# Cluster attention, then token mixing: every transfer on one queue, in order of time

## The chip, the cores and the metric

The kernel runs on one core of a Trainium2 chip. A core has a matrix engine (TensorE, PE in the profile), a vector engine (VectorE, DVE), a scalar engine (ScalarE, ACT), a general engine (GpSimd, POOL) and a sequencer for transfers (SyncE, SP). SP and ACT both issue DMA transfers in this program. The metric is the device time of one execution in microseconds (us), the median of several runs.

## The reference

```python
mask   = q_assign[:, :, :, None] == k_assign[:, :, None, :]   # nearest of 16 centroids
scores = where(mask, (q @ k.T) / sqrt(D), -1e9)               # B=4, H=8, S=768, D=64
x      = softmax(scores) @ v                                  # regrouped to (4, 768, 512)

theta  = x @ w_theta
zr, zi = x * cos(theta), x * sin(theta)
y      = w_tok_r @ zr + w_tok_i @ zi                          # over the 768 tokens
u      = x + y
out    = u + maximum(u @ w_ch, 0)
```

## The kernel before, in words

The kernel first computes attention, in 16 pairs of heads, and writes x, transposed, to DRAM (`xT_d[b]`). Then it does the token mixing batch by batch. A batch has 6 tiles of 128 tokens; tile number n = 6 b + t runs from 0 to 23. Every float32 matrix is split into a high and a low part, and a product is made of three matmuls.

For each tile there is a *theta*: `theta_parts` splits a column block `xs` of x into `xh` (ACT) and `xl`; `theta_angle` multiplies it by w_theta on TensorE (tile `tp`); `theta_turn` reduces the angle on VectorE (`kk`, `rab`), takes an Abs on ACT, transposes a block `xb` of x into `xn`, and starts the load of the next `xb` (`load_blocks`, four transfers of many short pieces); then come two sines on ACT and two products with `xn` on VectorE. `load_columns` loads the next `xs`.

Batches 0 and 1 are *plain* (`PLAIN = 2`): `mix` multiplies a tile of z by the tiles of the token weights, and `channel_plain` does the channel mix. While they run, `make_forms` loads the kept weights (`w_d`) into two buffers `ws`, makes for each of the 6 weight tiles seven sums of halves, splits each into a high and a low part in two other `ws` buffers, and writes them to DRAM (`w_f`, called wf).

Batches 2 and 3 use these sums: `mix_forms` makes seven products for a tile (m in the order 4, 3, 1, 5, 2, 6, 7), once for the first 256 columns of z (tiles 0 to 5) and once for the second (tiles 5 to 0). The seven sums of a weight tile have to lie in SBUF for it. Tiles 1 to 3 get places of the plain weights (`wr`, `wi`). Tile 0 gets the four `ws` buffers (m = 4, 3, 1, 5) and three plain places; tile 5 gets the same seven places after tile 0, tile 4 the four buffers `u` of the channel mix. So tiles 0, 4 and 5 are loaded again in every batch. `split_z` prepares z for it: VectorE makes three sums (`zt`) and a difference, ACT casts both parts to their high halves, POOL subtracts for the low halves (`zf`). The second half of z goes by DRAM: `keep_turned` writes it (`zd`), `load_z` reads it back (`zb`).

What sets the order: in the attention and in batches 2 and 3 the instructions of each engine stand in the order in which the code issues them (`in_order`). In the plain batches a scheduler orders them by its own estimate of time, and transfers of batch 2 can be moved in among those of the plain batches if their data allow it. An engine takes its instructions strictly in order, so a transfer that has to wait holds all behind it on its issuing engine, computing ones too if that is ACT. The transfers of SP and ACT share eight completion counters in turn: an issue also waits until the last transfer on its counter has landed.

Of the kernel before, what the change touches and what calls it, by code (L numbers as in the profile page):

```python
# [31 lines left out]
AHEAD = 2  # L32
# [9 lines left out]
def kernel(  # L42
# [19 lines left out]
    nc = tc.nc  # L62
    B, H, D, S = qT.shape
    P = 128
    NP = H // 2
    NT = S // P
    C = cent.shape[0] // H
    DM = w_theta.shape[0]
# [6 lines left out]
    xT_d = [dram.tile([P, NP, S], F32, name=f"xT_d{b}") for b in range(B)]  # L75
# [104 lines left out]
    w_d = {(t, x): dram.tile([P, S], F32, name=f"wd{t}{x}") for t in range(NT) for x in "ri"}  # L180
# [11 lines left out]
    for x in range(3):  # L192
        x = (NPAIR + x) % 3
# [67 lines left out]
    def f(ap):  # L261
        return ap.bitcast(F32)
# [60 lines left out]
    def turn_one_hot(pi, n):  # L323
        ot = bank(f"ot{pi}{n}").bitcast(BF16)[:, 0:S]
        for t in range(NT):
            nc.tensor.transpose(
                out=ot[:, t * P:(t + 1) * P], in_=ohp[:, n, t].rearrange("p j c -> p (j c)"), identity=identb)
        return ot
# [267 lines left out]
    def run(gen):  # L596
        for _ in gen:
            pass
# [29 lines left out]
    def behind(x):  # L628
        return tc.issue_after(x.ins) if x is not None else nullcontext()
# [8 lines left out]
    def load_blocks(n):  # L638
        if n == B * NT:
            return  # L640
        b, t = divmod(n, NT)
        xb = blocks[n] = ma[0].tile([P, DM], F32, tag="xb", name=f"xb{n}")


        for a in range(P // 32):
            src = xT_d[b][:, :, t * P + 32 * a:t * P + 32 * a + 32]
            (nc.sync if n < 2 else nc.scalar).dma_start(  # L647
                out=xb[32 * a:32 * a + 32].rearrange("c (n m r) -> c n m r", n=NP, m=P // 32),
                in_=src.rearrange("(m c) n r -> c n m r", c=32))

# [144 lines left out]
    while u <= NUT or todo:  # L795
# [8 lines left out]
        if 0 <= u < NUT:  # L804
            both(score_products, u, exps)
            if u == 0:
# [4 lines left out]
                for n, x in ((1, "mk"), (0, "mq")):  # L811
                    nc.scalar.activation(
                        out=st[1][x], in_=turn_one_hot(1, n), func=AF.Identity,
# [45 lines left out]
    spares = [spare_pool.tile([P, S], F32R, name=f"ws{x}") for x in range(3)]  # L859
# [19 lines left out]
    def load_x(b):  # L879
        xT = xts[b] = mx.tile([P, NP, S], F32, tag="xT", name=f"xT{b}")  # L880
        if b == 0:

            for p in range(NP):
                nc.sync.dma_start(out=xT[:, p], in_=xT_d[b][:, p])
        else:
            nc.sync.dma_start(out=xT, in_=xT_d[b])
# [31 lines left out]
    columns = {}  # L918

    def load_columns(n):  # L920

        b, t = divmod(n, NT)
        if 0 < b < B:
            columns[n] = mxs.tile([P, NCT, P], F32, tag="xs", name=f"xs{n}")
            with tc.issue_after(last_load[0].ins):
                nc.scalar.dma_start(out=columns[n], in_=xT_d[b][:, :, t * P:(t + 1) * P])

    PLAIN = 2
    turning = {}
# [31 lines left out]
    z_d = {}  # L961
# [13 lines left out]
    def keep_turned(b, t, rab):  # L975
        zs[b, t] = rab
        z_d[b, t] = dram.tile([P, 2, DM // 2], F32, tag=f"z{t}", name=f"zd{b}_{t}", bufs=2)
        nc.scalar.dma_start(out=z_d[b, t], in_=rab[:, :, DM // 2:DM])

    def rotate(b, t, rab, xn):  # L980
        if b < PLAIN:
# [20 lines left out]
    last_mix = [None]  # L1002
# [37 lines left out]
    HD = DM // 2  # L1040
# [7 lines left out]
    def make_forms():  # L1048

        for t in range(NT):  # L1050
            for x, k in enumerate("ri"):
                nc.sync.dma_start(out=f(spares[x]), in_=w_d[t, k])
            part = [f(spares[x])[:, c:c + HS] for x in range(2) for c in (0, HS)]
            yield
            for x, m in enumerate(ORDER):
                to = spares[2 + (7 * t + x) % 2]
                hi, lo = to[:, 0:HS], to[:, HS:S]
                p, op, q = W_SUM[m]
                src = part[p]
                if op is not None:  # L1060
                    src = mzb.tile([P, 2, HD], F32, tag="zb", name=f"sum{t}_{m}").rearrange("p x n -> p (x n)")[:, 0:HS]
                    nc.vector.tensor_tensor(out=src, in0=part[p], in1=part[q], op=op)
                nc.scalar.copy(out=hi, in_=src)  # L1063
                nc.gpsimd.tensor_tensor(out=lo, in0=src, in1=f(hi), op=ALU.subtract)  # L1064
                nc.sync.dma_start(out=w_f[t][:, m - 1], in_=f(to))
                yield

    def load_forms(t, ms=ORDER):
        for m in ms:
            nc.sync.dma_start(out=f(forms[t][m]), in_=w_f[t][:, m - 1])  # L1070
# [3 lines left out]
    def load_z(b, t):  # L1074

        if t >= 0:
            second[t] = mzb.tile([P, 2, HD], F32, tag="zb", name=f"zb{b}_{t}")
            nc.sync.dma_start(out=second[t], in_=z_d.pop((b, t)))

    def split_z(b, t, h):  # L1080

        src = zs.pop((b, t)) if h == 0 else second.pop(t)
        n = src.shape[2] // P
        z = mz.tile([P, 2, 2 * DM], F32R, tag="z", name=f"zf{b}_{t}_{h}")
        hi, lo = z[:, 0], z[:, 1]
        c, s = src[:, 0], src[:, 1]
        sums = mzt.tile([P, 3 * P], F32, tag="zt", name=f"zt{b}_{t}_{h}")
        nc.vector.tensor_tensor(out=sums[:, 0:HD], in0=c[:, 0:HD], in1=s[:, 0:HD], op=ALU.add)  # L1088
        nc.vector.tensor_tensor(out=sums[:, HD:3 * P], in0=c[:, 0:P], in1=s[:, P:HD], op=ALU.add)
        parts = src.rearrange("p x (m n) -> p (x m) n", n=P)  # L1090
        nc.vector.tensor_tensor(
            out=parts[:, 1:n + 1:n - 1], in0=src[:, :, P:HD], in1=src[:, :, 0:P], op=ALU.subtract)
        for cols, of in ((slice(0, 3 * P), sums), (slice(3 * P, 7 * P), src[:, :, 0:HD])):
            h_, l_ = (x[:, cols] for x in (hi, lo))
            if len(of.shape) == 3:
                h_, l_ = (x.rearrange("p (x n) -> p x n", x=2) for x in (h_, l_))
            nc.scalar.copy(out=h_, in_=of)  # L1097
            nc.gpsimd.tensor_tensor(out=l_, in0=of, in1=f(h_), op=ALU.subtract)  # L1098
        return hi, lo
# [101 lines left out]
    late_weights, new_forms = late(), make_forms()  # L1201
    for n in range(PLAIN * NT):
        b, t = divmod(n, NT)
        theta(*divmod(n + AHEAD, NT))
        if b == 0:
            weights_after[0] = splits[n + 1]
            next(late_weights, None)
        mix(b, t)
        if 0 < n < PLAIN * NT - 1 and t < NT - 1:
            for _ in range(5 if b == 0 else 6):  # L1210
                next(new_forms, None)
        if n == PLAIN * NT - 2:
            run(new_forms)
            load_forms(0)
            load_forms(1)
        if t == NT - 1:
            if b == PLAIN - 1:
                load_forms(2)
                load_forms(3)
            channel_plain(b)  # L1220
            load_x(b + 1)
    us = [u_tile(f"u{x}") for x in range(4)]
# [15 lines left out]
    def turn(n):  # L1238
        if n < last:
            theta_turn(n)  # L1240
            sines(turning[n][4])
# [7 lines left out]
    for b in range(PLAIN, B):  # L1249
        for t in range(NT - 1):  # L1250
            n = b * NT + t
            done(n + 1)
            angle(n + 2)
            before(n + 3)
            now, z = z, split_z(b, t + 1, 0)
            mix_forms([(t, now)], t == 0, False)
            if t < 4:
                load_forms(*((4, ORDER[:4]), (4, ORDER[4:]), (5, ORDER[:4]), (5, ORDER[4:]))[t])
            if t == 2 and b > PLAIN:
                load_x(b)  # L1260
            turn(n + 2)
            if t == NT - 2:
                load_z(b, 5)
        n = b * NT + NT - 1
        load_z(b, 4)
        done(n + 1)
        now, z = z, split_z(b, 5, 1)
        load_z(b, 3)
        mix_forms([(5, now)], False, True)
        angle(n + 2)  # L1270
        add_products(b, 0, 0)
        now, z = z, split_z(b, 4, 1)
        load_z(b, 2)
        add_products(b, 0, 1)
        before(n + 3)
        for t in (5, 4, 3, 2, 1, 0):
            mix_forms([(t, now)], t == 5, t == 0)
            if t == 5:
                load_forms(0, ORDER[:4])
            if t == 4:  # L1280
                load_forms(0, ORDER[4:])
            if t > 1:
                now, z = z, split_z(b, t - 2, 1)
                load_z(b, t - 4)
            else:
                now = z
            if t == 5:
                turn(n + 2)
            if t == 4:
                done(n + 2)  # L1290
                split_u_part(b, 0, us, nc.vector)
        for k in range(2):
            add_products(b, 1, k)
        split_u_part(b, 1, us, nc.vector)
        if b + 1 < B:
            z = split_z(b + 1, 0, 0)
        channel(b, us)
# [53 lines left out]
```

## Time and profile before

| | us |
|---|---|
| median of 3 runs (lowest, highest) | 856.79 (854.31, 858.82) |
| the profiled execution: its own time | 860.01 |
| its span, first to last instruction | 858.2 |
| mean granted TensorE clock | 0.958 |
| attention, up to its last row sums on TensorE | 0 to 451.4 |
| plain batches, from the first product of `mix` | 453.4 to 646 |
| batch 2 (theta 14 to the end of its channel mix) | 646 to 760.5 |
| batch 3 | 760.5 to 858.2 |

A line of the timeline gives start, duration, engine, line of the code, operation, output tile and input tiles, sizes and count. In square brackets stands how long the engine sat idle before, and what ended that. ACTq and SPq are the issuing of transfers by ACT and SP. PEclk, or "granted clock", is the share of its full clock that TensorE got. The lines that matter are shown in the prediction.

### The profile page before, as it was taken

The numbers are of one execution on the slowest core, as the hardware profiler recorded it, in microseconds if no ns is written. First come the engines' busy times: TensorE is split into PE (matmuls) and PEld (weight loads), VectorE is DVE, ScalarE is ACT, GpSimd is POOL, SyncE is SP. The second block draws the span as 40 slices with busy tenths as digits, with TensorE's granted clock in tenths as the row PEclk, the third lists the DMA queues.
The fourth block names the chain that finished last, engine by engine and source line by source line (L and its number), as shares of the span: only waits on it lengthen the run. The fifth ranks groups of instructions, "written<-read, shape, count | busy, mean of one in ns | idle before, by whom it ended". The sixth has DMA issues, their size and how long they took to land. (4 is left out here: it accounts for less than half of the span.)

```text
span 858.2 us, 14512 instructions
## 1 busy us (share of the span) xinstructions
PE 785.1 (91%) x5316; PEld 578.1 (67%) x5316; DVE 635.1 (74%) x797; ACT 415.0 (48%) x835; POOL 564.2 (66%) x345
## 2 busy tenths in 40 slices
PE   9999999999999999997999895999983969995798
PEld 6656666656656666664657784888872858994698
DVE  7688999999999999995858997474654357634654
ACT  3566667667667666663554445333522233213320
POOL 3677898899999998995664946835662244223350
PEclk9999999999999999998999998899986898897999
DMA  3113433334544334424537747489969646167242
GB/s 131 53 52 97 129 110 104 104 117 153 159 134 128 102 115 158 149 89 173 156 81 216 221 118 220 156 296 303 323 230 365 239 104 194 41 249 229 69 171 74
DMA packets 115235, 135.38 MB, mean 158 GB/s; under 512 B 62226, under 2 KB 81308, under 8 KB 114780
## 3 DMA queue, kind: packets, MB, share of 16 engines
q1 hardware_dynamic: 55932, 120.82, 41.6%
q10 hardware_dynamic: 59232, 13.64, 7.5%
q8 instruction: 42, 0.69, 0.3%
q14 instruction: 29, 0.24, 0.1%
HBM read 96.99 MB, written 37.33 MB: 157 GB/s over the span
## 5 line engine op out<-in xcount | busy, mean ns | idle before, releaser
L485 ACT ACTIVATE at<-sc 128x384 f32<-128x384 f32 x384 | 173.8, 493 | 100.4 <-PE m L409 53.2
L431 DVE TENSOR_REDUCE nm<-m 128x1 f32<-128x768 f32 x192 | 180.4, 947 | 29.9 <-PE m L409 23.9
L496 POOL TENSOR_TENSOR acc<-at,at 128x768 f32<-128x768 f32 x64 | 126.5, 1976 | 40.4 <-ACT at L485 40.4
L409 PE MATMUL m<-hk,hq 64*128 64x384 f32 x384 | 147.8, 385 | 0.2 <-DVE nm L431 0.2
L557 PE MATMUL av<-at,vt 128*64 128x384 f32 x768 | 146.7, 501 | 0.2 <-ACT xt L572 0.2
L496 POOL TENSOR_TENSOR acc<-acc,at 128x768 f32<-128x768 f32 x64 | 131.8, 2059 | 13.4 <-ACT at L485 11.4
L409 PE MATMUL m<-mk,mq 64*128 64x384 f32 x384 | 128.6, 335 | 0.1
L409 PE MATMUL sc<-hq,hk 64*128 64x384 f32 x384 | 117.4, 392 | 7.3 <-ACT at L485 7.1
L409 PEld LDWEIGHTS sc<-hq,hk 64*128 64x128 f32 x384 | 55.4, 184 | 69.7 <-ACT at L485 25.0
L409 PE MATMUL sc<-mq,mk 64*128 64x384 f32 x384 | 97.3, 336 | 0.0
L409 PE MATMUL sc<-hq,lk 64*128 64x384 f32 x384 | 97.3, 335 | 0.0
L409 PE MATMUL sc<-lq,hk 64*128 64x384 f32 x384 | 97.0, 335 | 0.0
L557 PEld LDWEIGHTS av<-at,vt 128*64 128x64 f32 x768 | 46.8, 136 | 59.6 <-issue 54.5
L1098 POOL TENSOR_TENSOR zf<-zt,zf 128x384 fp32r<-128x384 f32 x24 | 26.2, 1091 | 70.2 <-ACT zf L1097 65.1
L409 PEld LDWEIGHTS m<-hk,hq 64*128 64x128 f32 x384 | 70.8, 184 | 2.0 <-DVE nm L431 1.4
L409 PEld LDWEIGHTS m<-mk,mq 64*128 64x128 f32 x384 | 71.4, 186 | 0.8 <-DVE mk L374 0.4
L500 DVE TENSOR_TENSOR acc<-acc,acc 128x768 f32<-128x768 f32 x30 | 63.5, 2118 | 0.0
L1064 POOL TENSOR_TENSOR ws<-sum,ws 128x384 fp32r<-128x384 f32 x30 | 33.9, 1135 | 39.7 <-ACT ws L1063 39.6
L1025 PE MATMUL y<-wr_hi,z 128*128 128x512 f32 (+1 forms) x192 | 51.5, 340 | 4.6 <-ACT z L991 3.7
L409 PEld LDWEIGHTS sc<-mq,mk 64*128 64x128 f32 x384 | 54.6, 185 | 0.0
L409 PEld LDWEIGHTS sc<-lq,hk 64*128 64x128 f32 x384 | 54.5, 186 | 0.0
L409 PEld LDWEIGHTS sc<-hq,lk 64*128 64x128 f32 x384 | 54.4, 185 | 0.0
(222 smaller groups left out, 1779.1 us busy)
## 6 DMA issues: line engine op xcount, KB each, us to landing
wf<-ws SPq DMA_DIRECT2D x42, 384.0 KB
ws<-wf SPq DMA_DIRECT2D x20, 384.0 KB
vt<-in_v_dram SPq DMA_DIRECT2D x16, 384.0 KB
rb<-sd SPq DMA_DIRECT2D x32, 192.0 KB
xT_d<-xt SPq DMA_DIRECT2D x16, 384.0 KB
out_dram<-ot SPq DMA_DIRECT2D x32, 192.0 KB
rawq<-in_qT_dram SPq DMA_DIRECT2D x15, 384.0 KB
rawk<-in_kT_dram SPq DMA_DIRECT2D x15, 384.0 KB
```

The lines of the kernel that those rows point to most:

```text
L409: nc.tensor.matmul(out, lhsT=stat[r, cols], rhs=mov[r, over], start=start, stop=stop)
L431: nc.vector.tensor_reduce(out=s["nm", a][:, j, i // 2:i // 2 + 1], in_=s["m", j][:, :, 0:HS], op=ALU.max, axis=AX.XY, negate=True)
L485: last_exp[0] = nc.scalar.activation(out=s["at", a, i][:, j], in_=s["sc", j], func=AF.Exp, scale=SCALE)
L496: last_acc[0] = nc.gpsimd.tensor_tensor(out=s["acc", a, x], in0=prev, in1=at, op=ALU.add)
L500: nc.vector.tensor_tensor(out=s["acc", a, 0], in0=s["acc", a, 0], in1=s["acc", a, 1], op=ALU.add)
L557: nc.tensor.matmul(s["av"][64 * j:64 * j + 64], lhsT=s["vt"][:, i, j, :], rhs=s["at", a, i][:, j], start=(i == 0), stop=(i == NT - 1))
L1025: last_mix[0] = nc.tensor.matmul(y_at(d, c0, c1), lhsT=zz[:, d * P:(d + 1) * P], rhs=ww[:, c0:c1], start=first and lead, stop=last, skip_g ...
L1064: nc.gpsimd.tensor_tensor(out=lo, in0=src, in1=f(hi), op=ALU.subtract)
L1098: nc.gpsimd.tensor_tensor(out=l_, in0=of, in1=f(h_), op=ALU.subtract)
```

## The change

All transfers of the mixing are issued by SP: the blocks `xb`, the columns `xs` and the second half of z (`zd`) were issued by ACT before. The loads of the weights' sums are written tile by tile from the fourth tile of batch 1 on (tile 1, then 0 and 2, then 3), with the column loads ahead of them, and not all at its end. The loads of kept weights into the `ws` buffers are placed behind the last matmul issued by `mix` so far. In batches 2 and 3 the next theta's turn is written behind the load of z, and `split_z` handles the four parts of which the first products are made ahead of the three sums.

```diff
@@ load_blocks
-            (nc.sync if n < 2 else nc.scalar).dma_start(
+            nc.sync.dma_start(
@@ load_columns
-        if 0 < b < B:
+        if 0 < b < B and n not in columns:
...
-                nc.scalar.dma_start(out=columns[n], in_=xT_d[b][:, :, t * P:(t + 1) * P])
+                nc.sync.dma_start(out=columns[n], in_=xT_d[b][:, :, t * P:(t + 1) * P])
@@ keep_turned
-        nc.scalar.dma_start(out=z_d[b, t], in_=rab[:, :, DM // 2:DM])
+        nc.sync.dma_start(out=z_d[b, t], in_=rab[:, :, DM // 2:DM])
@@ make_forms
-                nc.sync.dma_start(out=f(spares[x]), in_=w_d[t, k])
+                with behind(last_mix[0]):
+                    nc.sync.dma_start(out=f(spares[x]), in_=w_d[t, k])
@@ split_z
-        for cols, of in ((slice(0, 3 * P), sums), (slice(3 * P, 7 * P), src[:, :, 0:HD])):
+        for cols, of in ((slice(3 * P, 7 * P), src[:, :, 0:HD]), (slice(0, 3 * P), sums)):
@@ the loop over the plain tiles
-        if n == PLAIN * NT - 2:
-            run(new_forms)
-            load_forms(0)
-            load_forms(1)
+        if b == PLAIN - 1:
+            if t == NT - 2:
+                run(new_forms)
+            if t > 2:
+                load_columns(n + AHEAD + 2)
+            if t == NT - 2:
+                load_forms(0)
+            if t > 2:
+                load_forms(t - 2)
         if t == NT - 1:
-            if b == PLAIN - 1:
-                load_forms(2)
-                load_forms(3)
             channel_plain(b)
@@ the loop over batches 2 and 3
-            turn(n + 2)
             if t == NT - 2:
                 load_z(b, 5)
+            turn(n + 2)
```

Three places show what this does to the order. The first is ACT in batch 2, from the Abs of theta 15 to the casts of z for tile 3 of the products. Before:

```order
L670 ACTIVATE rab_3_7870<-rab_3_7870 128x512
L647 DMA xb_7987<-xT_d_62 32x16x32 x4
L965 ACTIVATE rab_3_7870<-rab_3_7870 128x512
L965 ACTIVATE rab_3_7870<-rab_3_7870,halfpi 128x512
L978 DMA zd_3_7996<-rab_3_7870 256x1x256
L926 DMA xs_8011<-xT_d_63 128x4x128
L936 CAST xh_5_8014<-xs_7940 128x512
L1097 CAST zf_3_0_8020<-zt_3_0_8021 128x384
L1097 CAST zf_3_0_8020<-rab_3_7870 128x512
```

Now (the numbers of lines are one higher behind the changed place):

```order
L670 ACTIVATE rab_3_7870<-rab_3_7870 128x512
L965 ACTIVATE rab_3_7870<-rab_3_7870 128x512
L965 ACTIVATE rab_3_7870<-rab_3_7870,halfpi 128x512
L936 CAST xh_5_8014<-xs_7940 128x512
L1098 CAST zf_3_0_8020<-rab_3_7870 128x512
L1098 CAST zf_3_0_8020<-zt_3_0_8021 128x384
```

The six issues are gone from ACT, and the cast of the 512 columns stands ahead of the cast of the sums.

The second place is SP where batch 1 ends and batch 2 begins. wf_6124 to wf_6129 are the sums of weight tiles 0 to 5; ws_6084, 6085, 6086 and 6121 are the four buffers, for m = 4, 3, 1 and 5 of tile 0. Before:

```order
L1065 DMA wf_6129<-ws_6086 128x768
L1065 DMA wf_6129<-ws_6121 128x768
L1173 DMA out_dram<-ot_1_0_7782 128x384
L1070 DMA ws_6084<-wf_6129 128x768
L1173 DMA out_dram<-ot_1_1_7797 128x384
L1070 DMA ws_6085<-wf_6129 128x768
L1070 DMA ws_6086<-wf_6124 128x768
L1070 DMA ws_6121<-wf_6124 128x768
```

Now:

```order
L1066 DMA wf_6129<-ws_6121 128x768
L1174 DMA out_dram<-ot_1_0_7784 128x384
L1071 DMA ws_6086<-wf_6124 128x768
L1174 DMA out_dram<-ot_1_1_7799 128x384
L647 DMA xb_7916<-xT_d_62 32x16x32
L978 DMA zd_2_7925<-rab_2_7839 256x1x256
L926 DMA xs_7940<-xT_d_62 128x4x128
L1071 DMA ws_6121<-wf_6124 128x768
```

The two loads of tile 5 that stood ahead of tile 0's third and fourth load are further back, and zd and xs of theta 14 and 17 stand ahead of the fourth.

The third place is SP at the begin of batch 3. Before:

```order
L1173 DMA out_dram<-ot_1_3_8619 128x384
L1070 DMA u_7832<-wf_6128 128x768 x2
L1070 DMA u_7833<-wf_6128 128x768 x2
L1070 DMA u_7834<-wf_6128 128x768 x2
L1070 DMA u_7835<-wf_6128 128x768
L1070 DMA ws_6084<-wf_6129 128x768
L1070 DMA ws_6085<-wf_6129 128x768
```

Now:

```order
L1174 DMA out_dram<-ot_1_3_8619 128x384
L926 DMA xs_8635<-xT_d_63 128x4x128
L1071 DMA u_7834<-wf_6128 128x768 x2
L1071 DMA u_7835<-wf_6128 128x768 x2
L647 DMA xb_8683<-xT_d_63 32x16x32 x4
L978 DMA zd_2_8692<-rab_2_8280 256x1x256
L926 DMA xs_8707<-xT_d_63 128x4x128
L1071 DMA u_7836<-wf_6128 128x768 x2
L1071 DMA u_7837<-wf_6128 128x768
L647 DMA xb_8754<-xT_d_63 32x16x32 x4
L978 DMA zd_3_8763<-rab_3_8637 256x1x256
L1071 DMA ws_6084<-wf_6129 128x768
```

The loads of tiles 4 and 5 went out in one run before; now the small transfers of each theta stand between them, and zd holds what is behind it until VectorE has made its products.

## The prediction

> **What bounds the kernel now.** The page comes first: TensorE is busy 91% of the span, and nearly all that it lacks is in the last third. The windows, one for each stage of the last two batches, show where:
>
> ```profile
> PE 785.1 (91%) x5316; PEld 578.1 (67%) x5316; DVE 635.1 (74%) x797; ACT 415.0 (48%) x835; POOL 564.2 (66%) x345
> 646.00:671.00 25.00, 10.46 (x35) 8.66 (x34) 8.59 (x15) 3.64 (x7) 4.28 (x4) 0.60 1.04 373
> 671.00:713.00 42.00, 33.81 (x155) 29.88 (x155) 23.52 (x38) 14.24 (x25) 15.36 (x13) 0.91 0.46 127
> 713.00:760.50 47.50, 44.49 (x235) 43.34 (x234) 28.60 (x51) 12.15 (x21) 17.56 (x15) 0.93 0.42 128
> 760.50:796.40 35.90, 25.26 (x120) 22.50 (x120) 14.25 (x26) 9.09 (x17) 9.72 (x8) 0.86 0.76 251
> 796.40:858.20 61.80, 52.09 (x279) 49.03 (x277) 34.98 (x62) 13.79 (x24) 17.98 (x16) 0.97 0.30 106
> ```
>
> The columns are length, busy time of PE, PEld, DVE, ACT, POOL, granted clock, DMA share, GB/s. No engine is full in these stages, so waits set the time. Next the timeline of TensorE: the first five rows give the price of undisturbed work, the others are the stalls and edges (the last row is the end of the chain of waits).
>
> ```profile
> 736.59 0.68 PE L1113 MATMUL four<-wi_lo,zf 128*128 128x384 f32 x3
> 740.23 0.68 PE L1113 MATMUL four<-ws,zf 128*128 128x384 f32 x3
> 743.87 0.51 PE L1164 MATMUL four<-u,wch_hi 128*128 128x384 f32 x2
> 760.51 1.08 PE L659 MATMUL tp<-wth_hi,xh 128*128 128x512 f32 x4
> 763.27 0.69 PE L1113 MATMUL four<-ws,zf 128*128 128x384 f32 x3
> ...
> 655.46 1.33 PE L1113 MATMUL four<-ws,zf 128*128 128x384 f32 x3 [6.50 <-DMA ws<-wf]
> 665.71 2.67 PE L1113 MATMUL y<-ws,zf 128*128 128x384 f32 x6 [7.96 <-DMA ws<-wf]
> 668.18 1.17 PE L1113 MATMUL y<-wr_hi,zf 128*128 128x384 f32 x3
> 671.06 1.35 PE L659 MATMUL tp<-wth_hi,xh 128*128 128x512 f32 x4
> 684.36 1.17 PE L659 MATMUL tp<-wth_hi,xh 128*128 128x512 f32 x4
> 693.61 1.16 PE L659 MATMUL tp<-wth_hi,xh 128*128 128x512 f32 x4 [2.19 <-DVE rab L667]
> 728.52 0.62 PE L1113 MATMUL four<-wi_hi,zf 128*128 128x384 f32 x2 [1.73 <-ACT zf L1097]
> 784.17 2.08 PE L659 MATMUL tp<-wth_hi,xh 128*128 128x512 f32 x4 [10.64 <-ACT xh L936]
> 795.04 0.69 PE L1113 MATMUL four<-wr_lo,zf 128*128 128x384 f32 x3
> ...
> 534.00 1.01 PE L1164 MATMUL cp<-uh,wch_hi 128*128 128x384 f32 x2 [7.41 <-ACT uh L1156]
> ...
> 854.33 0.56 DVE ot L1171
> ```
>
> One tile's seven products cost 740.23 - 736.59 = 3.64 us, one theta (tp) 763.27 - 760.51 = 2.76, one channel mix 760.51 - 743.87 = 16.64. Against these, stage by stage:
> - 646.0 to 671.0: 25.0 us for a theta and one tile (6.4): 18.6 lost, to loads of the sums of weights (ws<-wf).
> - to 713.0: 42.0 for four thetas and five tiles (29.2): 12.8 lost.
> - to 760.5: 47.5 for a theta, six tiles, a channel mix (41.2): 6.3 lost.
> - to 795.04: 34.5 for four thetas and three tiles (22.0): 12.5 lost.
> - to TensorE's end, at 854.3: 59.3 for nine tiles and a channel mix (49.4): 9.9 lost. The output behind it ends at 858.2.
>
> That is 60 us. Now ScalarE in the second and fourth of these stages:
>
> ```profile
> 685.78 0.64 ACT L670 ACTIVATE rab<-rab 128x512 f32<-128x512 f32 x1 [1.08 <-DVE rab L668]
> 686.34 2.66 ACTq L647 DMA_DIRECT2D xb<-xT_d  x4
> 689.05 0.63 ACT L965 ACTIVATE rab<-rab 128x512 f32<-128x512 f32 x1 [2.62 <-DMA xb<-xT_d]
> ...
> 774.43 0.63 ACT L965 ACTIVATE rab<-rab 128x512 f32<-128x512 f32 x1 [8.02 <-DMA ws<-wf]
> 782.81 0.59 ACTq L926 DMA_DIRECT2D xs<-xT_d  x1
> 783.50 0.62 ACT L936 CAST xh<-xs 128x512 fp32r<-128x512 f32 x1 [7.83 <-DMA zd<-rab]
> ```
>
> ScalarE itself issues the transfers xb, zd and xs. The four xb stand between the Abs and the sines and take 2.66 us. Before 774 an issue also has to wait for a load of weights to land, so the sines start 8.02 late, and the next xh, behind zd and xs, another 7.83: the 10.64 us of TensorE at 784.
>
> **The change part by part.** *Issues moved from ACT to SP (xb, xs, zd).* Six DMA issues a tile leave ScalarE.
>
> Second stage: from theta to theta 693.61 - 684.36 = 9.25 us. Work alone would be 2.76 + 3.64 = 6.40; the loop of waits (VectorE's reduction, Abs, xb issue, sines, VectorE's products) is what takes 9.25. Less 2.66 it is 6.6, barely over TensorE. The issue of xs (0.59) and that of zd lie beside VectorE's work and are worth nothing by themselves. Four periods with some disturbance bring 42.0 to 33: -9, between 0 (the loop finds another wait) and -12.8 (TensorE full).
>
> Third stage: the one theta inside it loses its xb issue too, behind which the cast zf stood that TensorE waits for at 728.52. That stall is the stage's only long one, so -4 of 6.3; ends +2 (the zt buffer, below) and -6.3.
>
> Fourth stage: ScalarE no longer waits there for foreign transfers. The 10.64 and the slow matmuls behind (2.08 instead of 1.08) go: 34.5 to 23, -11.5, ends -5 (half of the wait remains as late xs) and -12.5.
>
> Fifth stage: after the last theta there is another path:
>
> ```profile
> 804.71 0.57 ACTq L978 DMA_DIRECT2D zd<-rab  x1
> 807.24 10.30 SPq L1078 DMA_DIRECT2D zb<-zd x4
> 809.95 0.43 DVE L1088 TENSOR_TENSOR zt<-zb 128x256 f32<-128x256 f32 x1 [4.20 <-DMA zb<-zd]
> ...
> 789.89 0.60 DVE kk L666
> 796.41 1.31 DVE rab L972 x2
> 797.82 0.43 DVE zt L1088
> ...
> 799.19 1.00 POOL L1098 TENSOR_TENSOR zf<-zt,zf 128x384 fp32r<-128x384 f32 x1 [4.94 <-ACT zf L1097]
> 800.16 1.26 POOL L1098 TENSOR_TENSOR zf<-rab,zf 128x512 fp32r<-128x512 f32 x1
> ```
>
> A tile's second half is written to DRAM (804.71 to 807.24, 2.5 us) and read back (2.7). The next three rows are of the chain of waits, the last two POOL's: from the reduction's start at 789.89 to the products' end 7.8 us, or 5.2 without the xb issue, then 3.6 for the split (797.82 to 801.42). From the end of the last theta this makes 5.2 + 5.2 + 3.6 = 14.0 us, or about 13.4 with the split's new order, and TensorE has three tiles, 10.9, to do meanwhile. So some 2.5 us appear here once the earlier gain uncovers them. -3 of 9.9, ends +4 and -9.9.
>
> All these issues, 2.66 and 0.57 and 0.59, are 3.8 us more on SP for each theta, ten times in these stages, beside some 21 loads of weights a batch at 0.6 (below, 1.84 for three). Of a batch's 90 to 100 us SP has the room; what matters is what it waits for (rivals).
>
> *Order of the loads of weights' sums.* In the first stage SP and ACT did this:
>
> ```profile
> 657.69 0.57 SPq L1070 DMA_DIRECT2D ws<-wf  x1
> 659.00 1.84 SPq L1070 DMA_DIRECT2D ws<-wf  x3
> 655.17 0.51 ACT L1063 CAST ws<-sum 128x384 fp32r<-128x384 f32 x1 [2.91 <-DMA ws<-wf]
> 652.65 2.47 ACTq L647 DMA_DIRECT2D xb<-xT_d  x3
> ```
>
> Before, two loads for tile 5 (ws<-wf 5, which wait for TensorE's first products) stand ahead of the third and fourth load of tile 0 that TensorE needs next. Now they come later, and of tile 4's loads four instead of seven stand ahead. But the fourth load of tile 0 now stands behind zd_2 and xs, so behind the sines of theta 14. Those follow the last cast (655.17), which stood behind three xb issues (2.47): about 653 now, and the sines right after. Products 653 to 655, the write and load issues to 658, 2.5 us to land (as the zd above): 660.5; then four products at the slow rate, 0.96 each (three from 668.18 to 671.06, at a granted clock of 0.60 in this stage): about 665 instead of 671.06. -6, ends 0 (the DMA engines are full, share 1.04, and the backlog is the same) and -12.
>
> *Parts in the order of the products.* POOL now splits the 512 columns (1.26) first, then the 384 (1.00). The first product (m = 4) needs the 512; it no longer waits for 1.00 but starts about 0.4 later, since VectorE's difference comes ahead: -0.6 a tile where TensorE waits for POOL, and the zt buffer is free 1.3 later. Both are inside the ranges above; taken as nothing.
>
> *Loads behind last_mix, and the plain batches.* Sums are made later, ScalarE has fewer issues. The one stall of size, 7.41 at 534.00, loses perhaps 2 us of ACT's issues and gains a sum ahead (0.5): -1.5, ends +6 (SP holds an xb) and -7.
>
> Sum: 6 + 9 + 4 + 11.5 + 3 + 1.5 = 35 us. The profiled execution took 860.0 (span 858.2), so 825; the median before, 856.8, is 3.2 below that execution, so **822 us**.
>
> The Trainium skill, "DMA: Bandwidth & Descriptors", section "Issuing engines are not separate DMA queues", holds that issuing from several engines only saves the sequencer's time, usually little. By it the terms that rest on the issue (9, 4, 11.5) would all but go, and the sum be about 10: 847. The trace disagrees here: the issue stands inside a loop of 9.25 us and takes 2.66 of it, and up to 8.02 when held up.
>
> **The rivals.**
> *Slower: the small transfers stand behind the big ones.* On one queue, xb (needed by VectorE's transpose in the same loop) goes behind loads of weights issued just before. The rate when the engines are full is 373 GB/s, so a load of 128 x 768 words (0.39 MB) is 1.05 us. Behind them stand: xb after 4, 3, 4, 3 and (with xT, 1.57 MB by its 128 x 3072 words) 8 such loads, 23 us; the zb of either batch after 4, twice, 17 us. If nothing hid these 40 us, they would eat the 35: 862. It decides when seven eighths of this is uncovered. Against it: each xb is issued a period, over 6 us, ahead of its transpose. The Trainium skill, "DMA: Bandwidth & Descriptors", section "Queues, rings and completion order", says that a DMA engine alternates between queue rows packet by packet, which speaks for this rival: on one row that turn-taking is gone. No run shown here has the small transfers on SP's queue in these stages.
>
> *Half: another wait takes the place of the issue.* If half of the 2.66 comes back, as waiting for a late xb or for VectorE and POOL, the loop stays near 8. Then the five stages give -3, -4, -2, -5 and 0, the plain batches -1: -15, 842.
>
> *No change.* ScalarE's wait of 8 us is for the landing of loads, and SP inherits the waiting: it issues in order and the DMA engines carry the same bytes. 857, within 0.5% (4.3 us), which is about what a measurement here can tell from nothing.
>
> **Chances.** The forecast's mechanism, 806 to 836: 0.62. Half, 837 to 852: 0.20. No change: 0.07. Slower: 0.11. So faster 0.82, same 0.07, slower 0.11; range 806 to 848, since the low end needs nearly all terms at their good ends, and most of the half case belongs in.
>
> **What would show it.** Right: no DMA issue on ACT; theta to theta 6.4 to 7 us in batches 2 and 3; no wait of 10 us for xh; the first tile's second stall ends about 660; a wait of some 2 us for zb in batch 3. Wrong: VectorE's transposes or ACT's xh waiting for xb or xs; SP waiting for DVE or POOL with loads behind it that TensorE waits for; TensorE waiting for z in the first plain batch.

## The result, and the profile after

The changed kernel takes 833.82 us (median of 3 runs, 832.49 to 834.28) against 856.79: a ratio of 0.973, 95% interval 0.9685 to 0.9775. The profiled execution is the median one, with a span of 832.1 us.

First the line of engines and that of the transfer queues from the page of the changed kernel (packets, MB, share of 16 DMA engines); then its windows, one for each of the five stages, with the columns as before.

```profile
PE 777.1 (93%) x5316; PEld 572.7 (69%) x5316; DVE 639.5 (77%) x797; ACT 414.1 (50%) x835; POOL 564.4 (68%) x345
q1 hardware_dynamic: 115164, 134.45, 50.8%
```

```profile
637.59:661.60 24.01, 10.48 (x35) 8.67 (x34) 9.19 (x15) 3.44 (x7) 4.36 (x4) 0.61 1.00 350
661.60:692.76 31.16, 30.62 (x155) 27.80 (x154) 23.29 (x33) 13.19 (x23) 14.29 (x11) 0.98 0.67 183
692.76:742.02 49.26, 44.92 (x236) 41.82 (x235) 31.63 (x56) 13.21 (x23) 19.65 (x16) 0.97 0.45 135
742.02:764.06 22.04, 22.04 (x113) 20.01 (x112) 17.71 (x27) 9.50 (x17) 10.28 (x8) 1.00 0.86 238
764.06:828.15 64.09, 55.50 (x286) 52.08 (x284) 32.74 (x61) 13.46 (x24) 19.20 (x16) 0.92 0.47 161
```

ACT's queue is gone from the page: all of the kernel's own transfers are on q1. TensorE's busy time fell by 8 us with the same number of matmuls, since fewer of them ran at a low clock (mean granted clock 0.966 against 0.958). The second and fourth stage, 42 and 34.5 us before, are now 31.2 and 22.0, and the fourth has no gap at all. But the third and fifth are longer than before (47.5 and 59.3). The timeline of TensorE shows the thetas of batch 2, one of batch 3 and the stalls left:

```profile
644.75 1.33 PE L1114 MATMUL four<-ws,zf 128*128 128x384 f32 x3 [4.25 <-DMA ws<-wf]
652.00 1.30 PE L1114 MATMUL y<-ws,zf 128*128 128x384 f32 x3 [4.95 <-DMA ws<-wf]
657.62 1.30 PE L1114 MATMUL y<-ws,zf 128*128 128x384 f32 x3 [4.33 <-DMA ws<-wf]
661.60 1.80 PE L659 MATMUL tp<-wth_hi,xh 128*128 128x512 f32 x4
668.74 1.09 PE L659 MATMUL tp<-wth_hi,xh 128*128 128x512 f32 x4
675.17 1.08 PE L659 MATMUL tp<-wth_hi,xh 128*128 128x512 f32 x4
681.59 1.09 PE L659 MATMUL tp<-wth_hi,xh 128*128 128x512 f32 x4
...
761.30 1.08 PE L659 MATMUL tp<-wth_hi,xh 128*128 128x512 f32 x4
...
777.99 1.01 PE L1114 MATMUL four<-ws,zf 128*128 128x384 f32 x2 [5.77 <-ACT zf L1098]
```

Theta to theta is 6.4 us (7.1 once), which is TensorE's own work. The 10.64 us wait for xh is gone. New is the 5.77 us stall at 777.99. VectorE and SP show where it comes from:

```profile
774.04 0.71 DVE L652 STREAM_TRANSPOSE xn<-xb 128x512 f32<-128x512 f32 x1 [5.27 <-DMA xb<-xT_d]
782.08 0.42 DVE L1089 TENSOR_TENSOR zt<-zb 128x256 f32<-128x256 f32 x1 [4.87 <-DMA zb<-zd]
...
760.60 2.00 SPq L1071 DMA_DIRECT2D ws<-wf  x4
762.65 0.64 SPq L886 DMA_DIRECT2D xT<-xT_d  x1
763.39 6.24 SPq L647 DMA_DIRECT2D xb<-xT_d  x4
```

The last xb is issued behind four loads of sums and the 1.57 MB of xT; its issue takes 6.24 us instead of the usual 2.63, and VectorE waits 5.27 us for it.

### The profile page after: what moved, and what is told of

It is laid out like the page before. It is cut to its first block, busy times and chain, and to the rows that moved or that the text cites. A ratio compares the mean times of both kernels' runs of the same rounds, so it can differ in the third digit from the quotient of the medians.

```text
span 832.1 us, 14509 instructions
## 1 busy us (share of the span) xinstructions
PE 777.1 (93%) x5316; PEld 572.7 (69%) x5316; DVE 639.5 (77%) x797; ACT 414.1 (50%) x835; POOL 564.4 (68%) x345
## 5 line engine op out<-in xcount | busy, mean ns | idle before, releaser
L431 DVE TENSOR_REDUCE nm<-m 128x1 f32<-128x768 f32 x192 | 180.2, 947 | 29.7 <-PE m L409 24.1
L1099 POOL TENSOR_TENSOR zf<-rab,zf 128x512 fp32r<-128x512 f32 x12 | 16.3, 1355 | 53.8 <-ACT zf L1098 53.8
L1025 PE MATMUL y<-wr_hi,z 128*128 128x512 f32 (+1 forms) x192 | 50.3, 340 | 1.4 <-POOL z L993 1.1
L1065 POOL TENSOR_TENSOR ws<-sum,ws 128x384 fp32r<-128x384 f32 x30 | 34.4, 1150 | 24.6 <-ACT ws L1064 22.3
```

Source lines behind the costliest of these rows:

```text
L431: nc.vector.tensor_reduce(out=s["nm", a][:, j, i // 2:i // 2 + 1], in_=s["m", j][:, :, 0:HS], op=ALU.max, axis=AX.XY, negate=True)
L1025: last_mix[0] = nc.tensor.matmul(y_at(d, c0, c1), lhsT=zz[:, d * P:(d + 1) * P], rhs=ww[:, c0:c1], start=first and lead, stop=last, skip_g ...
```

## The experiments

Medians and ratios to the kernel before, measured beside it on the same chip in each group (runs 1 to 4, 5 to 8, 9 to 11, and 12); the changed kernel was measured only with the result, so it is compared with these runs by the ratios. Stage lengths are from one profiled execution each; the first column is the time from the last long wait of attention on TensorE (401.11 in the kernel before, 399.66 in the changed one) to theta 14, the last one that from theta 23's end to TensorE's end.

| kernel | median us | ratio, 95% | plain | 1 | 2 | 3 | 4 | 5 |
|---|---|---|---|---|---|---|---|---|
| before | 856.8 | 1 | 244.9 | 25.0 | 41.9 | 47.6 | 34.5 | 59.3 |
| changed | 833.8 | 0.973 (0.9685-0.9775) | 237.9 | 24.0 | 31.2 | 49.3 | 22.0 | 64.1 |
| 1: before, all three issues on SP | 833.8 | 0.9715 (0.9666-0.9765) | 239.5 | 22.0 | 31.7 | 51.1 | 22.1 | 60.3 |
| 2: changed, issues on ACT | 858.0 | 1.0001 (0.9983-1.002) | 243.7 | 24.9 | 40.1 | 49.2 | 37.3 | 58.7 |
| 3: changed, xT behind xb | 831.7 | 0.9686 (0.9641-0.9732) | 239.2 | 22.5 | 30.4 | 48.5 | 22.0 | 62.2 |
| 4: changed, old split order | 831.5 | 0.9689 (0.964-0.9737) | 239.9 | 22.8 | 31.9 | 46.4 | 22.1 | 60.1 |
| 5: changed, xT two tiles earlier | 832.2 | 0.9706 (0.9657-0.9754) | 240.1 | 22.7 | 31.5 | 46.6 | 22.1 | 63.0 |
| 6: before, only xb on SP | 832.5 | 0.9697 (0.9664-0.9731) | 243.1 | 21.1 | 32.5 | 49.0 | 22.1 | 60.1 |
| 7: before, only xs and zd on SP | 855.6 | 0.9958 (0.9938-0.9977) | 247.1 | 18.8 | 42.6 | 50.3 | 29.7 | 59.0 |
| 8: changed, 4 and 5 together | 831.5 | 0.9697 (0.9655-0.9739) | 237.2 | 22.7 | 31.9 | 48.7 | 22.0 | 60.0 |
| 9: changed, order by half | 829.7 | 0.9677 (0.9648-0.9705) | 239.0 | 22.1 | 30.4 | 49.5 | 22.0 | 61.3 |
| 10: changed, no DRAM for tile 5 | 827.3 | 0.9631 (0.9606-0.9655) | 237.8 | 21.9 | 30.4 | 47.4 | 22.0 | 60.6 |
| 11: changed, 9 and 10 together | 828.4 | 0.9649 (0.9625-0.9673) | 238.8 | 22.3 | 31.3 | 49.5 | 22.0 | 59.2 |
| 12: changed, 10 and 3 together | 824.4 | 0.9622 (0.9595-0.9648) | 238.0 | 22.7 | 30.5 | 48.0 | 22.1 | 58.3 |

**Which edit made the gain: runs 1 and 2.** The first gives the kernel before the three `nc.sync` lines alone, the second takes them out of the changed kernel:

```diff
-            (nc.sync if n < 2 else nc.scalar).dma_start(     # xb
+            nc.sync.dma_start(
-                nc.scalar.dma_start(out=columns[n], ...      # xs
+                nc.sync.dma_start(out=columns[n], ...
-        nc.scalar.dma_start(out=z_d[b, t], ...               # zd
+        nc.sync.dma_start(out=z_d[b, t], ...
```

> The kernel before, with nothing changed but the issuer: xb, xs and zd go out on SP; loads of sums, kept weights and the split stay as before. Theory (the issue inside ScalarE's loop was the bound of the theta periods in batches 2 and 3): the second and fourth stage give the 10.7 and 12.5 us that they gave in the full change, theta to theta is 6.4 to 7.1 us, no long wait for xh; in the plain batches ScalarE is relieved just the same, so several of their 8.5 us appear too: about 830 to 838 us. Rival (the other edits made the gain, SP inherits the wait): theta to theta stays at 8 us or more, or a wait for xb or ws of like size takes the place of the issue, and the time is 850 us or more. A third way, the gain in batches 2 and 3 is there but the plain batches need the later sums: 837 to 845.

> The changed kernel, with xb (from the third on), xs and zd issued by ACT again; all else of the change stays. Theory: theta to theta goes back to 9 us in batch 2, and the wait for a foreign landing of 7 us or more comes back on ScalarE in batch 3; the two stages lose 23 us, the third and fifth get back up to 6: 845 to 858 us. Rival (later sums and loads tile by tile made the gain): 830 to 840 us.

The issues alone give 833.8 us, all of the gain; without them nothing is left (1.0001). The loads written tile by tile, the kept weights behind last_mix and the order of split_z are together worth nothing that these runs can tell. In run 2 ScalarE waits as it did before:

```profile
763.40 0.63 ACT L670 ACTIVATE rab<-rab 128x512 f32<-128x512 f32 x1 [1.60 <-DVE rab L668]
766.53 6.59 ACTq L647 DMA_DIRECT2D xb<-xT_d  x4
773.17 0.63 ACT L965 ACTIVATE rab<-rab 128x512 f32<-128x512 f32 x1 [9.14 <-DMA ws<-wf]
781.91 0.59 ACTq L926 DMA_DIRECT2D xs<-xT_d  x1
782.60 0.62 ACT L936 CAST xh<-xs 128x512 fp32r<-128x512 f32 x1 [8.19 <-DMA zd<-rab]
```

The sines stand behind the xb issue, and an issue behind the landing of an older transfer: 9.14 us, then 8.19 for xs.

**Which of the issues: runs 6 and 7** (one line, or the other two, of the diff above, on the kernel before).

> The kernel before, with only xb issued by SP; xs and zd stay on ACT. Theory of the prediction (xb's issue of 2.66 us stands in the loop, xs and zd lie beside VectorE's work): the second stage gets all of its 10 us; the fourth stage gets about half of its 12.5, since xs and zd on ACT still wait for foreign landings; plain batches get their 5 us: 836 to 844 us. Rival (any DMA issue left on ACT holds it by a foreign landing): less than half of the 24 us, 846 us or more. Second rival (xb alone is everything): 831 to 836.

> The kernel before, with only xs and zd issued by SP; xb stays on ACT. Theory: the second stage keeps its theta to theta of 9 us, the plain batches gain nothing, the fourth stage still has sines late behind an xb issue that waits for a foreign landing (8 us), but not the second 8 us in front of xh; 848 to 856 us. Rival (xs and zd were what held ScalarE): 845 us or less.

xb alone is everything (0.9697 against 0.9715 for all three); the second rival was right and the theory too low by half of the fourth stage, which got all of its 12.4 us. With xs and zd on ACT but xb gone, no issue of theirs was held in batches 2 and 3. Run 7 gained 0.4%; the hold of 8 us behind the xb issue, which its theory expected in the fourth stage, did not come. TensorE's thetas in its batch 2, and an Abs, an issue and a sine of batch 3:

```profile
679.82 1.16 PE L659 MATMUL tp<-wth_hi,xh 128*128 128x512 f32 x4 [0.87 <-DVE rab L667]
690.25 2.04 PE L659 MATMUL tp<-wth_hi,xh 128*128 128x512 f32 x4 [3.78 <-DVE rab L667]
...
774.33 0.63 ACT L670 ACTIVATE rab<-rab 128x512 f32<-128x512 f32 x1 [2.50 <-DVE rab L668]
774.89 2.63 ACTq L647 DMA_DIRECT2D xb<-xT_d  x4
777.56 0.63 ACT L965 ACTIVATE rab<-rab 128x512 f32<-128x512 f32 x1 [2.60 <-DMA xb<-xT_d]
```

A period of 10.4 us stays, with the 2.63 us of issue in the loop. So the 8-us holds of the fourth stage needed all three on ACT; they went when either part left, and the 2.6 us when xb left.

**The longer fifth stage: runs 3 and 5.** `load_x(b)` for batch 3 moves behind `turn(n + 2)`, in run 3 at t = 2, in run 5 at t = 0:

```diff
-            if t == 2 and b > PLAIN:
-                load_x(b)
             if t == NT - 2:
                 load_z(b, 5)
             turn(n + 2)
+            if t == 2 and b > PLAIN:      # run 5: t == 0
+                load_x(b)
```

> The changed kernel, with batch 3's load of xT (1.57 MB) issued behind the turn of theta 22, so behind the issue of xb for theta 23, and not ahead of it. Theory (the fifth stage's loss is xb standing behind xT): VectorE's wait of 5.27 us for xb before the transpose of theta 23 is 1 us or less, TensorE's stall of 5.77 behind it goes with it, 3 to 6 us less: 828 to 831 us. Rival A (the four loads of tile 5's sums and the full DMA engines hold xb, not xT): the wait stays at 3 us or more, time within 1.5 us of the changed kernel's. Rival B (xT then lies ahead of zd and zb): the wait moves to zb of tile 5, which is later, time the same.

> The changed kernel, with batch 3's load of xT issued behind the turn of theta 20, two tiles earlier than in the changed kernel. Theory (what stands behind the 1.57 MB waits for them, first xb, and with xT one place later zd and zb): with xT out of the way of both, xb lands in time and the wait for zb of tile 5 falls from 8.5 us (xT behind the turn of theta 22) to 3 to 4.5 us; the fifth stage falls from 64.1 to 59 to 61 us, the fourth stays at 22: 828 to 831 us. Rival A: xT now holds xb of theta 22 in the fourth stage, which gets longer by 2 us or more: no gain. Rival B: the wait for zb is the loads of tile 5's sums and the way through DRAM, not xT, and stays above 5 us.

Neither moved the time by what a median of these runs can tell: 0.9686 and 0.9706 against 0.973, intervals overlapping. VectorE's waits, of run 3 first and then of run 5:

```profile
779.32 0.43 DVE L1089 TENSOR_TENSOR zt<-zb 128x256 f32<-128x256 f32 x1 [8.49 <-DMA zb<-zd]
```

```profile
765.06 0.71 DVE L652 STREAM_TRANSPOSE xn<-xb 128x512 f32<-128x512 f32 x1 [5.02 <-DMA xb<-xT_d]
771.99 0.71 DVE L652 STREAM_TRANSPOSE xn<-xb 128x512 f32<-128x512 f32 x1 [1.12 <-DMA xb<-xT_d]
779.87 0.42 DVE L1089 TENSOR_TENSOR zt<-zb 128x256 f32<-128x256 f32 x1 [4.70 <-DMA zb<-zd]
```

The wait belongs to whatever small transfer stands behind xT: zb of tile 5 in run 3 (8.49 instead of 4.87 us), xb of theta 22 in run 5 (5.02). On one queue, moving xT alone only chooses the victim. Rival B of run 3 was right on the mechanism; in run 5 the wait for zb stayed at 4.7, so that part is mostly the way through DRAM itself (zd is issued at 774.13, zb at 777.21, and VectorE goes on at 779.87). How long xb itself is waited for differs between executions: in runs 9, 10 and 11, whose order of issues in batch 3 is that of the changed kernel up to it, it is 4.00, 4.69 and 3.51 us instead of 5.27, and in run 4, with the same place of xT and the old split, 2.06.

**The split's order: runs 4, 8 and 9.** Run 4 puts the sums first again, run 8 does so with run 5's xT, run 9 only in the second half:

```diff
-        for cols, of in ((slice(3 * P, 7 * P), src[:, :, 0:HD]), (slice(0, 3 * P), sums)):
+        both = ((slice(3 * P, 7 * P), src[:, :, 0:HD]), (slice(0, 3 * P), sums))
+        for cols, of in both if h == 0 else both[::-1]:     # run 4: always both[::-1]
```

> The changed kernel, with split_z handling the three sums ahead of the four parts, as before the change. Theory of the prediction (the order is worth about nothing): within 2 us of the changed kernel. Rival A (the first product waits 0.6 us longer for POOL in each tile): up to 6 us slower, about 840. Rival B (the single zt buffer now is free 1.3 us later, and that is why the third stage lost 1.7 us): the third stage is 1 to 3 us shorter, 831 to 833.

> The changed kernel with xT behind the turn of theta 20 and the three sums of split_z ahead of the four parts, as before. If the fifth stage's loss was xT and the order of the split is worth nothing, the time is that of the kernel with xT early alone, within 2 us; if the old order is worth the 2.3 us that its median suggested, it is 2 us below that one.

> The changed kernel, with the order of split_z chosen by half: the four parts first in the first half of the columns (as the change has it), the three sums first in the second half (as before). Theory: with the parts first POOL lets go of the single zt buffer last, so from one tile's sums (zt) to the next it is 4.11 us in the second half against 3.33 with the sums first, and TensorE needs 3.64; this is what lengthened the third and fifth stage. Then the spacing of zt falls to 3.3 to 3.7, the fifth stage to 60 to 62 us, the third by up to 2: 829 to 832 us. Rival (what the order gives in one place it loses in another): within 1 us of the changed kernel's time.

VectorE at the start of the second half, in the changed kernel and then in run 4:

```profile
782.08 0.42 DVE L1089 TENSOR_TENSOR zt<-zb 128x256 f32<-128x256 f32 x1 [4.87 <-DMA zb<-zd]
786.20 0.42 DVE L1089 TENSOR_TENSOR zt<-zb 128x256 f32<-128x256 f32 x1 [0.37 <-POOL zf L1099]
790.31 0.43 DVE L1089 TENSOR_TENSOR zt<-zb 128x256 f32<-128x256 f32 x1 [0.36 <-POOL zf L1099]
```

```profile
778.91 0.42 DVE L1089 TENSOR_TENSOR zt<-zb 128x256 f32<-128x256 f32 x1 [4.64 <-DMA zb<-zd]
782.58 0.42 DVE L1089 TENSOR_TENSOR zt<-zb 128x256 f32<-128x256 f32 x1
786.24 0.41 DVE L1089 TENSOR_TENSOR zt<-zb 128x256 f32<-128x256 f32 x1
```

With the parts first the tiles follow each other in 4.11 us, held by POOL's last use of the one zt buffer; with the sums first in 3.66, TensorE's pace. The fifth stage agrees in the table: 60.0 to 60.3 us in the four kernels with xb on SP and the sums first (1, 4, 6, 8), 62.2 to 64.1 in the three with the parts first and tile 5 by DRAM (changed, 3, 5), and 61.3 in run 9, which has the sums first in this half. What the new order saves lies in the first half: the second stage is 30.4 to 31.5 us with it and 31.7 to 32.5 without. In the median it is a wash: 0.9689 and 0.9697 against 0.973 and 0.9706. Run 9 has 0.9677; its interval overlaps with those.

**A better version: runs 10, 11 and 12.** In run 10 the second half of tile 5 is split from the buffer in which VectorE made it, and tile 5's zd and zb are left out; run 11 adds run 9's order, run 12 puts xT behind the turn as in run 3:

```diff
+        if t < NT - 1:
-        nc.sync.dma_start(out=z_d[b, t], in_=rab[:, :, DM // 2:DM])
+            nc.sync.dma_start(out=z_d[b, t], in_=rab[:, :, DM // 2:DM])
...
-            if t == NT - 2:
-                load_z(b, 5)
...
+            src, at = (whole, 0) if h == 0 else (whole[:, :, HD:DM], 2)
```

> The changed kernel, with the second half of tile 5 taken straight from the buffer of z and not written to DRAM and read back (no zd, no zb for tile 5). Theory: VectorE's wait for zb of tile 5 (4.87 us in the fifth stage) is gone, and TensorE's gap between the halves with it: the fifth stage 2 to 4 us shorter, the whole 829 to 832 us. Rival: TensorE's gap was set by the late z of tile 5 in the first half (xb behind xT), and the second half starts late all the same: within 1 us.

> The changed kernel with both: the split's order chosen by half, and no way through DRAM for tile 5. If both act and add: 825 to 830 us. If one covers the other: as the better of the two alone.

> The kernel without the way through DRAM for tile 5, with xT issued behind the turn of theta 22 as well, so behind xb of theta 23. Alone, xT behind the turn only moved the wait from xb (5.27 us) to zb of tile 5 (8.49 us); with no zb of tile 5 there is nothing left there to wait. Theory: VectorE's wait for xb (4.69 us) and TensorE's stall of 5.2 us go, and no wait for zb of more than 2 us takes their place: the fifth stage 58 us or less (it is about 60.6 now), the whole 822 to 826 us. Rival: the wait moves once more, to zb of tile 4 or to a load of tile 5's sums behind xT, and the time stays at 826 to 829 us.

VectorE's wait for the last xb, in run 10 and in run 12:

```profile
768.02 0.71 DVE L652 STREAM_TRANSPOSE xn<-xb 128x512 f32<-128x512 f32 x1 [4.69 <-DMA xb<-xT_d]
```

```profile
767.69 0.71 DVE L652 STREAM_TRANSPOSE xn<-xb 128x512 f32<-128x512 f32 x1 [1.90 <-DMA xb<-xT_d]
```

Run 10 takes 827.3 us; its interval (0.9606 to 0.9655) lies below the changed kernel's. Run 11 adds nothing to it. Run 12, with the last xb ahead of xT and no zb of tile 5 behind it, takes 824.4 us, the fastest here, in the range of its theory, and the fifth stage is 58.3. The wait for xb, which its theory had go, fell only to 1.90 us. Run 12's interval overlaps with run 10's, so the further 3 us are likely and not proven.

## Why the prediction was right, and where its terms were off

Forecast 822 us, measured 833.8: the likeliest case (806 to 836) came true, near its slow end. The mechanism held in the second and fourth stage; the four other terms were -14.5 us together and measured -3.0. The terms, in the profiled spans (the spans differ by 26.1 us, TensorE's end by 26.1):

| term | forecast | measured | |
|---|---|---|---|
| second stage | -9 | -10.7 | right |
| fourth stage | -11.5 | -12.5 | right |
| first stage | -6 | -1.0 | wrong cause |
| third stage | -4 | +1.7 | wrong sign |
| fifth stage | -3 | +4.8 | wrong sign |
| plain batches | -1.5 | -8.5 | too small |

*Second and fourth stage.* "Less 2.66 it is 6.6, barely over TensorE" is what the thetas show (6.43), and run 6 with xb alone has it too. That xs and zd "are worth nothing by themselves" holds for the second stage (run 7: 42.6 us). The page of the Trainium skill that the prediction weighed, "DMA: Bandwidth & Descriptors", section "Issuing engines are not separate DMA queues", would have put the sum at about 10 us; the move of one issuer, run 6, measured 26.7 us beside 859.2.

*First stage and plain batches, together.* From the attention's mark to theta 15 the change saved 8.0 us, against 7.5 forecast, but the steps were wrong, so that this sum came out is luck. The first stage was put down to the order of the loads. Run 1 keeps the old code for the loads and has 22.0 us there; run 2 has the new code and 24.9. The plain batches were judged by their one long stall, which grew (7.41 to 10.52 us); what shrank were periods earlier in these batches. Two thetas of TensorE before, with its longest wait between them and the start of ScalarE's xb issues there, then the same two thetas after:

```profile
475.88 1.07 PE L659 MATMUL tp<-wth_hi,xh 128*128 128x512 f32 x4
481.52 0.62 PE L1025 MATMUL y<-wr_hi,z 128*128 128x512 f32 x2 [2.75 <-ACT z L991]
482.99 0.56 ACTq L647 DMA_DIRECT2D xb<-xT_d  x1
490.30 1.09 PE L659 MATMUL tp<-wth_hi,xh 128*128 128x512 f32 x4
```

```profile
472.09 1.08 PE L659 MATMUL tp<-wth_hi,xh 128*128 128x512 f32 x4
483.24 1.08 PE L659 MATMUL tp<-wth_hi,xh 128*128 128x512 f32 x4
```

14.42 us became 11.15. It is xb's issuer that does this: run 6 has 11.16 there, run 7 14.28 (473.33 to 484.49 and 474.16 to 488.44). How is open: the wait of 2.75 us ends before the xb issue of this period begins, and the scheduler's order in these batches changed as well (in run 6 the cast of wr_hi stands ahead of the Abs of this period, before behind it). Of the 8.0 us run 1 gets 8.4, run 2 1.3, run 6 5.7 and run 7 4.0, in one execution each. The kernels that share the changed kernel's code up to theta 15 (the changed one, 3 to 5 and 8 to 12) differ by 3.1 us among themselves, so it is the issues again, xb among them (the period above), and xs and zd likely too. About 1.5 us more of the plain term is attention that ended earlier in this execution.

*Third stage.* The step was that the stall at 728.52 came from an xb issue ahead of the cast and that the stage would lose 4 us with it, "the stage's only long one". The first half holds: that tile's products (those with wi_hi) have no such wait in the changed kernel nor in run 1. The second half failed. The two tiles behind it now wait three times 0.7 us for ACT and POOL (in run 1 1.17 us each, for POOL), and a new wait of 1.39 us for VectorE's sums of products appears; three of these rows:

```profile
699.63 0.79 PE L1114 MATMUL y<-ws,zf 128*128 128x384 f32 x3 [1.39 <-DVE xT L1123]
720.63 0.62 PE L1114 MATMUL four<-ws,zf 128*128 128x384 f32 x2 [0.73 <-ACT zf L1098]
721.98 0.44 PE L1114 MATMUL four<-ws,zf 128*128 128x384 f32 x1 [0.73 <-POOL zf L1099]
```

TensorE's idle time in the stage rose from 3.0 to 4.3 us. How long the stage is depends on such waits and on whether they slow the clock (below), and both differ from one execution to the next: it is 46.6 to 49.3 us in the changed kernel and runs 3 and 5, whose code there is the same, 46.4 and 48.7 in runs 4 and 8, which share theirs, 51.1 in run 1 at a clock of 0.93, and 49.5 in run 9 at a clock of 1.00, where the theory of run 9 had it shorter. So its sign is not settled.

*Fifth stage.* The window before, beside that of the changed kernel above:

```profile
795.04:854.29 59.25, 53.45 (x286) 50.38 (x284) 34.42 (x61) 14.45 (x25) 17.98 (x16) 0.97 0.32 109
```

Of the 4.8 us more, 2.8 are idle time of TensorE and 2.0 busy time, at a clock of 0.92 instead of 0.97. Two steps failed. The small transfers behind the big ones, the rival at 11%, happened at one of its places, "with xT ... 8 such loads": 5.27 us for xb. It was priced as a case by itself and not as a part of the likeliest case, which lost by it perhaps 2 us: run 3, where xb has no wait, is 1.9 us shorter in this stage although zb waits longer, in one execution each. With the issues alone (run 1) VectorE waits 2.53 us for this xb and TensorE 3.44 behind it, so the stage is 60.3 and not shorter than before. And "the zt buffer is free 1.3 later ... taken as nothing": in the second half that makes VectorE's and POOL's loop 4.11 us, more than TensorE's 3.64. From the first zt of that half to the sixth it is 22.1 to 22.7 us in the changed kernel and runs 3 and 5, and 20.1 to 20.7 in runs 1, 4, 6, 8 and 9, so this term, put at nothing, is some 2 us.

## What to carry to other kernels

A DMA issue costs the time of the engine that issues it: 2.6 us for four issues inside a loop of 9 us, and up to 9 when an issue waits for an older landing; look for issuing rows between the rows of a computing engine that is in a loop with the bottleneck. On one queue in order of time, look for the largest transfer and for the small one that stands next behind it, and take away the need for the small one rather than only move the large (run 12 did both). A buffer of which there is one ties the loop to its last reader, so the order of two readers matters where the loop is near the bottleneck's pace.

## What the runs showed of the hardware

A short stall of TensorE can cost a second time by the granted clock, and the same stall does not always. In run 1 a gap of 2.51 us at the start of the second half is followed by over 6 us at half the clock; in run 6 a gap of 2.51 us one tile earlier leaves it at full. The gap and windows of 3 us behind it, run 1 and then run 6 (columns as before):

```profile
699.12 0.98 PE L1113 MATMUL four<-ws,zf 128*128 128x384 f32 x2 [2.51 <-DVE xT L1122]
699.70:702.70 3.00, 2.30 (x8) 1.90 (x7) 2.90 (x8) 1.15 (x3) 1.61 (x2) 0.50 0.29 62
702.70:705.70 3.00, 3.00 (x11) 3.00 (x10) 3.00 (x6) 0.40 (x1) 2.92 (x3) 0.50 0.16 51
705.70:708.70 3.00, 3.00 (x18) 3.00 (x18) 2.93 (x6) 1.03 (x2) 1.42 (x2) 1.00 0.92 302
```

```profile
693.31 0.45 PE L1113 MATMUL four<-ws,zf 128*128 128x384 f32 x1 [2.51 <-POOL zf L1098]
693.80:696.80 3.00, 3.00 (x19) 3.00 (x18) 0.61 (x2) 0.00 (x0) 0.00 (x0) 1.00 0.81 168
```

In 3 us at half the clock TensorE made 11 matmuls instead of 18. The Trainium skill, "TensorE: Matmul & The Clock Gate", section "Part 1: The HAM clock gate", puts this down to a free-running window of about 3.4 us; half the clock and the difference between like stalls agree with it. It names a whole idle window for the slow state; the gap of 2.51 us in run 1 is shorter.

Which transfer held which is in the semaphores of the trace. Before, the loads of sums of tiles 4 and 5 go out one behind the other on SP, and each of the four xb issues behind 767 starts when the load eight issues back, on the same counter, has landed: at 767.44, 769.63, 771.58 and 773.82, the landings at 767.38, 769.61, 771.56 and 773.80. The xs at 782.81 waits in the same way for the xb of 769.63, which lands at 782.74. In runs 6 and 7 the small transfers on SP part these loads into groups of three or four, and when an issue on ACT comes in the fourth stage, the last transfer on its counter has already landed: in run 7 at 757.16 to 762.88 for the four xb issues from 764.40 on, in run 6 at 752.01 for the zd at 754.98.
